# Edges behind a unit's latest add or operand for attention, rotation and weight pieces, and units' own steps issued first

## The chip, the cores and the metric

One core of a Trainium2 chip runs the whole program. The time is device microseconds of one execution. TensorE (PE) does the matrix products, VectorE (DVE) and ScalarE (ACT) the elementwise work, GpSimd (POOL) some of it and some transfers, and SyncE (SP) issues the other transfers. Each of these engines has its own list of instructions, fixed when the program is built, and works it off in that order.

## What is computed

Attention without a softmax, an RMS norm, a mixer that turns each value by an angle and mixes over tokens, and a two-part MLP, for 8 batches of 576 tokens with 512 features:

```python
kv = np.einsum('bhsd,bhse->bhde', k, v)
out = np.einsum('bhsd,bhde->bhse', q, kv)
x = out / np.sqrt(np.mean(out * out, axis=-1, keepdims=True) + 1e-06) * g_norm
...
theta = x @ w_theta
zr, zi = x * np.cos(theta), x * np.sin(theta)
y = einsum('ts,bsd->btd', w_tok_r, zr) + einsum('ts,bsd->btd', w_tok_i, zi)
u = x + y
u = u + np.maximum(u @ w_ch, 0.0)
...
h = np.maximum(u.transpose(0, 2, 1) @ w_tok1, 0.0) @ w_tok2
u = u + h.transpose(0, 2, 1)
out = u + np.maximum(u @ w_ch1, 0.0) @ w_ch2
```

## The kernel before

Every float32 product is made of three float16 products: both operands are split into a high part (`hi`, made by ACT) and a low part (`lo`, made by DVE from the value and `hi`), and `mm3` (L82 to L84) multiplies high by high, high by low and low by high into one PSUM bank.

The first 640 us go batch by batch. For a batch b the pieces are `attend(o, r)` for five row blocks r (attention output, norm, and the transposed copy that a DMA on SP's queue makes from `xs` into `xt`), `rotate(o, r)` (the angle product into `pt`, three sine steps on ACT with `cs`, the product of `cs` with x on DVE at L362, then `zh` on ACT and `zl` on DVE at L365 and L367; the fifth block, `rotate_last`, goes by `zt` and a DMA), then the units, which PE works on without a break: eight of `mix` (M, banks `py`, each followed by an add on DVE at L422, `uh` on ACT at L423 and `ul` on DVE at L426), eight of `channel` (C, banks `pr`, reading `uh` and `ul`; an add on DVE at L448, `xs` on ACT at L449 and on DVE at L456, and every second unit a transposing DMA `xt<-xs` at L460), four of `token1` (H, banks `ph`, reading that `xt`) and eight of `token2` (T, banks `pu`). A bank named py513 belongs to batch 5, second chunk of tokens (320 columns), fourth block of features. After that a blocked MLP (L82 to L84 with `pa` to `nc`) runs to the end; nothing in it is touched.

While the units of batch b run, the attention and rotation pieces of batch b+1 are strewn between them, and so are weight pieces: a float64 weight comes as pairs of 32-bit words, which ACT and three DVE steps turn into float32 (`decode`, L128 to L130), and `stash` splits it (L215, L217) and stores it.

The pieces are Python generators. `go` issues the first step of a new unit or piece after one further step of all that are pending. The framework's scheduler then decides the place of each instruction on its engine by its own timeline of costs, dependences and priorities. `urgent()` gives a unit's own adds and operands a higher priority; dependences of the kind NoSync order two instructions of one engine without a semaphore.

Of the kernel before, what the change touches and what calls it, by code (L numbers as in the profile page):

```python
# [13 lines left out]
AF = mybir.ActivationFunctionType  # L14
ALU = mybir.AluOpType
AX = mybir.AxisListType
# [12 lines left out]
def attn_mixer_kernel(  # L29
# [38 lines left out]
        nc.vector.scalar_tensor_tensor(lo, src, scale, hi, ALU.mult, ALU.subtract)  # L68

    def split_relu(hi, lo, src):  # L70
        nc.scalar.activation(hi, src, AF.Relu)
        nc.vector.scalar_tensor_tensor(lo, src, 0.0, hi, ALU.max, ALU.subtract)

    def urgent():

# [44 lines left out]
    def decode(val, raw):  # L120

        bits = val.bitcast(I32)
        first = nc.scalar.activation(val, raw[..., 1].bitcast(F32), AF.Copy, scale=2.0**-112)
        if wp:

            tc.keep_in_program_order(first)
        yield
        nc.vector.tensor_scalar(bits, bits, 3, None, ALU.logical_shift_left)  # L128
        nc.vector.scalar_tensor_tensor(bits, raw[..., 0], 29, bits, ALU.logical_shift_right, ALU.bitwise_or)
        nc.vector.scalar_tensor_tensor(bits, raw[..., 1], -(2**31), bits, ALU.bitwise_and, ALU.bitwise_or)  # L130

    def weight(pool, w, src, part, n, hi, lo, scale, name, raw=None):

# [52 lines left out]
    def stash(w, name, row, cols, dst):  # L186

        w, k = words(w)  # L190
        raw = wp[0].tile([P, 4, P, 2], I32, tag="raw", name=f"{name}r")
        if k == 1:
            raw = raw.rearrange("p x n w -> p x (n w)").bitcast(F32)[:, :, :P]
        for x, half in ((0, w.shape[1] // 2), (2, 0)):
            at = half + k * cols
            src = w.rearrange("(i r) n -> r i n", i=2)[row:row + P, :, at:at + k * P]
            load(raw[:, x:x + 2] if k == 1 else raw[:, x:x + 2].rearrange("p x n w -> p x (n w)"), src)

        for _ in range(7):
            yield  # L200
        t = wp[0].tile([P, 8, P], F32, tag="st", name=f"{name}s")
        if k == 1:
            nc.scalar.activation(t[:, :4], raw, AF.Copy)
        else:
            yield from decode(t[:, :4].rearrange("p x n -> p (x n)"), raw.rearrange("p x n w -> p (x n) w"))
        yield
        nc.gpsimd.tensor_tensor(t[:, 5], t[:, 0], t[:, 1], ALU.add)
        nc.gpsimd.tensor_tensor(t[:, 7], t[:, 0], t[:, 2], ALU.subtract)
        nc.gpsimd.tensor_tensor(t[:, 6], t[:, 5], t[:, 2], ALU.subtract)
        nc.gpsimd.tensor_tensor(t[:, 4], t[:, 3], t[:, 6], ALU.subtract)  # L210

        for _ in range(3):
            yield
        hi, lo = (wp[0].tile([P, 7, P], F16, tag=f"st{i}", name=f"{name}{i}", bufs=1) for i in range(2))
        tc.keep_in_program_order(nc.scalar.activation(hi, t[:, 1:], AF.Copy, scale=SW))  # L215
        yield
        nc.vector.scalar_tensor_tensor(lo, t[:, 1:], SW, hi, ALU.mult, ALU.subtract)  # L217
        yield
        yield
        for d, src in zip(dst, (hi, lo)):  # L220
            nc.gpsimd.dma_start(d, src)
# [61 lines left out]
    def attend(o, r):  # L283
# [13 lines left out]
        xt = o.xt[r] = fp.tile([P, 2, KD, P], F16, tag="xt", name=f"xt{b}{r}", bufs=NR + 1)  # L297

        x3 = x.rearrange("p (h d) -> p h d", d=D)
        yield  # L300
        nc.scalar.activation(x3, po3, AF.Square, scale=D**-0.5)
        yield
        nc.vector.tensor_reduce(ss, x3, axis=AX.X, op=ALU.add)
        nc.gpsimd.tensor_tensor(ss, ss, eps, ALU.add)
        nc.gpsimd.tensor_tensor(ri, ss, mhalf, ALU.pow)  # L305
        nc.gpsimd.tensor_tensor(
# [1 line left out]
        )  # L308
        yield
        yield  # L310
        nc.vector.tensor_tensor(x3, po3, x3, ALU.mult)
        n = SR if r == NR else P
        R = o.R[:, :, r * P:r * P + n]
        if b == 0:
# [6 lines left out]
            split(xt[:, 0], xt[:, 1], px, 1.0)  # L321
            nc.scalar.activation(R, px[:, :, :n], AF.Copy, scale=SW)
            return
        nc.scalar.activation(xs[:, 0, :], x, AF.Copy)
        yield
        nc.vector.tensor_tensor(xs[:, 1, :], x, xs[:, 0, :], ALU.subtract)  # L326
        nc.sync.dma_start_transpose(xt.rearrange("p a k t -> p (a k) t"), xs.rearrange("p a d -> p (a d)"))
        yield
        yield
        nc.scalar.activation(R, xt[:, 0, :, :n], AF.Copy, scale=SW)  # L330
        yield
        nc.vector.scalar_tensor_tensor(R, xt[:, 1, :, :n], SW, R, ALU.mult, ALU.add)

    def prepare(o):
        if o.zh is None:
# [4 lines left out]
    def rotate(o, r):  # L340

        b = o.b
        if r == 0:
            prepare(o)
        zh, zl, x, xt = o.zh, o.zl, o.x[r], o.xt[r]
        if r == NR:
            yield from rotate_last(o, xt)
            return
        pt = bank(f"pt{b}{r}")
        mm3(pt, [(xt[:, 0, kk, :], xt[:, 1, kk, :], wth[:, kk, :], wtl[:, kk, :]) for kk in range(KD)])  # L350

        cs = fp.tile([P, 2, DM], F32, tag="cs", name=f"cs{b}{r}", bufs=2)
        f, sn = cs[:, 0], cs[:, 1]
        yield
        nc.scalar.activation(f, pt, AF.Copy, bias=MAGIC)
        nc.vector.scalar_tensor_tensor(f, f, MAGIC, pt, ALU.subtract, ALU.subtract)
        yield
        nc.scalar.activation(sn, f, AF.Sin, scale=-RAD)
        nc.scalar.activation(f, f, AF.Abs)
        nc.scalar.activation(f, f, AF.Sin, bias=hpi, scale=-RAD)  # L360
        yield
        nc.vector.tensor_tensor(cs, cs, x.unsqueeze(1).to_broadcast([P, 2, DM]), ALU.mult)  # L362
        yield
        at = slice(r, r + NR + 1, NR)
        nc.scalar.activation(zh[:, at, :], cs, AF.Copy)  # L365
        yield
        nc.vector.tensor_tensor(zl[:, at, :], cs, zh[:, at, :], ALU.subtract)  # L367

    def rotate_last(o, xt):


        b = o.b
        pt = bank(f"pt{b}{NR}")[:, :KD * SR].rearrange("p (k t) -> p k t", k=KD)
        for dt in range(KD):
            ds = slice(dt * P, (dt + 1) * P)
            mm3(pt[:, dt, :], [(wth[:, kk, ds], wtl[:, kk, ds], xt[:, 0, kk, :SR], xt[:, 1, kk, :SR]) for kk in range(KD)])
        cs = fp.tile([P, 2, DM], F32, tag="cs", name=f"cs{b}{NR}", bufs=2)
        f = cs[:, 0, :KD * SR].rearrange("p (k t) -> p k t", k=KD)
        sn = cs[:, 1, :].rearrange("p (k i t) -> p k i t", k=KD, i=2)
        zt = fp.tile([P, 2, DM], F16, tag="xs", name=f"zt{b}", bufs=2)  # L380
        yield
        nc.scalar.activation(f, pt, AF.Copy, bias=MAGIC)
        nc.vector.scalar_tensor_tensor(f, f, MAGIC, pt, ALU.subtract, ALU.subtract)
        yield
        nc.scalar.activation(sn[:, :, 1, :], f, AF.Sin, scale=-RAD)
        nc.scalar.activation(f, f, AF.Abs)
        nc.scalar.activation(sn[:, :, 0, :], f, AF.Sin, bias=hpi, scale=-RAD)
        R = o.R[:, :, SM:]
        for i in range(2):
            nc.vector.scalar_tensor_tensor(sn[:, :, i, :], R, 1.0 / SW, sn[:, :, i, :], ALU.mult, ALU.mult)  # L390
        yield
        sn = sn.rearrange("p k i t -> p (k i t)")
        nc.scalar.activation(zt[:, 0, :], sn, AF.Copy)
        yield
        nc.vector.tensor_tensor(zt[:, 1, :], sn, zt[:, 0, :], ALU.subtract)
        nc.sync.dma_start_transpose(
            o.zh[:, KM - 1:, :].rearrange("p i (k d) -> p (i k) d", k=KD), zt.rearrange("p i n -> p (i n)")
        )


    def mix(o, c, dt):
# [17 lines left out]
        yield  # L419
        u = R[:, dt, cols]  # L420
        with urgent():
            nc.vector.tensor_tensor(u, py[0], u, ALU.add)  # L422
            nc.scalar.activation(uh[:, dt, :], u, AF.Copy, scale=1.0 / SW)  # L423
        yield
        with urgent():
            nc.vector.scalar_tensor_tensor(ul[:, dt, :], u, 1.0 / SW, uh[:, dt, :], ALU.mult, ALU.subtract)  # L426

    def channel(o, c, ct):
        b, R = o.b, o.R
# [15 lines left out]
        yield  # L445
        x2 = R[:, ct, cols]
        with urgent():
            nc.vector.scalar_tensor_tensor(x2, pr, 0.0, x2, ALU.max, ALU.add)  # L448
            nc.scalar.activation(xs[:, ct % 2, :n], x2, AF.Copy, scale=1.0 / SW)  # L449
        yield  # L450
        lows = [(slice(tiles * P, None), slice(0, 2 * P))]
        if n > 2 * P:
            lows.append((slice(n, tiles * P), slice(2 * P, n)))
        with urgent():
            for dst, at in lows:
                nc.vector.scalar_tensor_tensor(xs[:, ct % 2, dst], x2[:, at], 1.0 / SW, xs[:, ct % 2, at], ALU.mult, ALU.subtract)  # L456

            if ct % 2:
                m = tiles + 2
# [216 lines left out]
        return nxt  # L676


    pending = []

    def go(unit):
        advance()
        next(unit)
        pending.append(unit)

    def advance():
        for g in list(pending):
            try:
                next(g)
            except StopIteration:  # L690
                pending.remove(g)

    def flush():
        while pending:
            advance()

    extra = []
# [35 lines left out]
    TOKEN1 = [f"H{c}{i}" for c in range(2) for i in range(KJ)]  # L733
    UNITS = {"M": mix, "C": channel, "H": token1, "T": token2}

    def run(units, o, nxt, after, beside):

        for u in units:
            kind, c, i = u[0], int(u[1]), int(u[2])
            if kind == "K":  # L740
                front(kv, after, c)
            else:
                go(UNITS[kind](o, c, i))
            for what in beside.get(u, "").split():
                if what == "w":
                    spare()
                elif what == "l":
# [134 lines left out]
```

## Time and profile before

| | us |
|---|---|
| median of 3 runs | 1137.32 (1134.44 to 1139.80) |
| the profiled execution | 1135.75 |
| its span in the trace | 1134.0 |
| PE busy | 1078.6 (95%) |
| DVE busy | 839.6 (74%) |
| ACT busy | 563.0 (50%) |
| POOL busy | 231.9 (20%) |

The span reaches from the first instruction to the last one; the execution's time is 1.75 us more than that. The busy share is a mean over the start, the eight batches and the long MLP at the end, so it has to be read by stretches of time. The granted clock of PE is given as a share of 2.4 GHz: 1.00 is 2.4 GHz and 0.50 is 1.2 GHz.

### The profile page before, as it was taken

The numbers are of one execution on the slowest core, as the hardware profiler recorded it, in microseconds if no ns is written. First come the engines' busy times: TensorE is split into PE (matmuls) and PEld (weight loads), VectorE is DVE, ScalarE is ACT, GpSimd is POOL, SyncE is SP. The second block draws the span as 40 slices with busy tenths as digits, with TensorE's granted clock in tenths as the row PEclk, the third lists the DMA queues.
The fourth block names the chain that finished last, engine by engine and source line by source line (L and its number), as shares of the span: only waits on it lengthen the run. The fifth ranks groups of instructions, "written<-read, shape, count | busy, mean of one in ns | idle before, by whom it ended". The sixth has DMA issues, their size and how long they took to land.

```text
span 1134.0 us, 21659 instructions
## 1 busy us (share of the span) xinstructions
PE 1078.6 (95%) x8884; PEld 817.8 (72%) x8884; DVE 839.6 (74%) x1475; ACT 563.0 (50%) x958; POOL 231.9 (20%) x290
## 2 busy tenths in 40 slices
PE   3879999999998989989999999999999999999998
PEld 3556776676875767667677777777777777777776
DVE  4998777897887887978836494867768585848584
ACT  3766536355455464653623363636354544546361
POOL 2441052462652824527100000000000000000000
PEclk9789999999999999999999999999999999999999
DMA  9535474776747647763292802011010202020101
GB/s 323 201 129 112 108 198 107 213 185 138 210 121 201 179 116 201 170 152 102 45 279 53 310 1 84 2 42 43 32 53 17 69 12 74 12 74 1 43 1 42
DMA packets 146083, 126.35 MB, mean 111 GB/s; under 512 B 93184, under 2 KB 121984, under 8 KB 145984
## 3 DMA queue, kind: packets, MB, share of 16 engines
q1 hardware_dynamic: 140608, 104.53, 33.7%
q0 software_dynamic: 5376, 20.45, 5.1%
q8 instruction: 69, 1.13, 0.4%
q14 instruction: 30, 0.25, 0.1%
HBM read 74.29 MB, written 29.88 MB: 92 GB/s over the span
## 4 chain that ended last, share of the span: by engine, by line
PE 60%; DVE 20%; DMA 8%; ACT 6%; issue 3%; POOL 1%; SPq 1%; ACTq 0%; DVEq 0%
PE na L82 4%; PE na L84 4%; PE na L83 4%; PE pa L84 4%; PE pa L83 4%; PE pa L82 4%; DMA xt<-xs 4%; DVE xs L326 2%; PE nc L82 2%; PE nc L83 2%; PE pc L84 2%; PE pc L83 2%; PE pc L82 2%; PE nc L84 2%; DVE cs L362 2%
## 5 line engine op out<-in xcount | busy, mean ns | idle before, releaser
L82 PE MATMUL py<-wmh,zh 128*128 128x256 f16 (+1 forms) x576 | 166.3, 289 | 7.4 <-ACT zh L365 3.9
L83 PE MATMUL py<-wml,zh 128*128 128x256 f16 (+1 forms) x576 | 166.0, 288 | 0.0
L84 PE MATMUL py<-wmh,zl 128*128 128x320 f16 (+1 forms) x512 | 146.5, 289 | 3.9 <-DVE zl L367 3.9
L84 PE MATMUL na<-gh,wbl 128*128 128x288 f16 x384 | 109.3, 286 | 0.0
L83 PE MATMUL pa<-o,wah 128*128 128x288 f16 x384 | 109.2, 286 | 0.0
L83 PE MATMUL na<-gl,wbh 128*128 128x288 f16 x384 | 109.1, 286 | 0.0
L82 PE MATMUL pa<-o,wah 128*128 128x288 f16 x384 | 108.4, 286 | 0.0
L84 PE MATMUL pa<-o,wal 128*128 128x288 f16 x384 | 107.8, 286 | 0.0
L82 PE MATMUL na<-gh,wbh 128*128 128x288 f16 x384 | 106.0, 286 | 0.2
L82 PE MATMUL pr<-uh,wch 128*128 128x256 f16 (+1 forms) x256 | 75.9, 297 | 8.7 <-ACT uh L423 8.7
L566 DVE TENSOR_TENSOR gl<-sum,gh 128x1152 f16<-128x1152 f32 x48 | 65.0, 1354 | 21.9 <-ACT gh L565 21.9
L83 PE MATMUL pr<-ul,wch 128*128 128x256 f16 (+1 forms) x256 | 75.9, 296 | 5.4 <-DVE ul L426 5.3
L83 PEld LDWEIGHTS <-wbh 128*128 128x128 f16 x672 | 65.7, 98 | 17.8 <-issue 0.9
L82 PEld LDWEIGHTS <-wah 128*128 128x128 f16 x672 | 65.8, 98 | 16.6
L82 PEld LDWEIGHTS <-wbh 128*128 128x128 f16 x672 | 65.7, 98 | 16.6
L84 PEld LDWEIGHTS <-wal 128*128 128x128 f16 x672 | 65.8, 98 | 16.6
L83 PEld LDWEIGHTS <-wah 128*128 128x128 f16 x672 | 65.8, 98 | 16.6
L84 PEld LDWEIGHTS <-wbl 128*128 128x128 f16 x672 | 65.7, 98 | 16.6
L84 PE MATMUL pr<-uh,wcl 128*128 128x256 f16 (+1 forms) x256 | 76.1, 297 | 0.0
L82 PEld LDWEIGHTS <-zh 128*128 128x128 f16 x576 | 57.0, 99 | 24.4 <-ACT zh L365 4.8
L305 POOL TENSOR_TENSOR ri<-ss,mhalf 128x8 f32<-128x8 f32 x40 | 72.0, 1801 | 1.4
L83 PEld LDWEIGHTS <-zh 128*128 128x128 f16 x576 | 57.0, 99 | 15.9
(292 smaller groups left out, 2917.4 us busy)
## 6 DMA issues: line engine op xcount, KB each, us to landing
q<-in_q SPq DMA_DIRECT2D x8, 1152.0 KB, 7.8
c<-u2d SPq DMA_DIRECT2D x32, 288.0 KB, 4.2
out<-c SPq DMA_DIRECT2D x64, 144.0 KB, 1.8
k<-in_k SPq DMA_DIRECT2D x24, 256.0 KB, 5.7
v<-in_v SPq DMA_DIRECT2D x24, 256.0 KB, 6.0
wa_r<-in_w_ch SPq DMA_DIRECT2D x24, 256.0 KB, 3.7
wb_r<-in_w_ch SPq DMA_DIRECT2D x24, 256.0 KB, 3.9
wad<-wa POOLq DMA_DIRECT2D x24, 224.0 KB, 2.6
```

Of the source, the lines that this page charges most:

```text
L82: nc.tensor.matmul(acc, ah, bh, start=first and i == 0, stop=False, **more)
L83: nc.tensor.matmul(acc, ah, bl, start=False, stop=False, **more)
L84: nc.tensor.matmul(acc, al, bh, start=False, stop=last and i == n - 1, **more)
L305: nc.gpsimd.tensor_tensor(ri, ss, mhalf, ALU.pow)
L326: nc.vector.tensor_tensor(xs[:, 1, :], x, xs[:, 0, :], ALU.subtract)
L362: nc.vector.tensor_tensor(cs, cs, x.unsqueeze(1).to_broadcast([P, 2, DM]), ALU.mult)
L566: nc.vector.tensor_tensor(h.lo[:, 3:], h.s, h.hi[:, 3:], ALU.subtract)
```

## The change

Two small helpers are added. `lead` remembers, for each engine, the latest instruction that is a unit's own add or operand (L422, L423, L426, L448, L449, L456 and the relu of `token1`). `placed` gives an instruction a NoSync edge behind the one that `lead` remembers on the same engine. Pieces of attention and rotation of the batches after the first, and the weight pieces of all, go through `placed`. In `advance`, the units' own steps (`leading`) are issued before those of the pieces (`pending`), and pieces of the batches after the second yield once or twice more. No instruction is added or removed.

```diff
     def split_relu(hi, lo, src):
-        nc.scalar.activation(hi, src, AF.Relu)
-        nc.vector.scalar_tensor_tensor(lo, src, 0.0, hi, ALU.max, ALU.subtract)
+        lead(nc.scalar.activation(hi, src, AF.Relu))
+        lead(nc.vector.scalar_tensor_tensor(lo, src, 0.0, hi, ALU.max, ALU.subtract))
+
+    last = {}
+
+    def lead(ins):
+
+        last[ins.ins.engine] = ins.ins
+        return ins
+
+    def placed(ins):
+
+        prev = last.get(ins.ins.engine)
+        if prev is not None:
+            tc.add_manual_dep(
+                ins.ins, prev.name,
+                mybir.DependencyInfo(mybir.DependencyClass.NoSync, mybir.DependencyReason.DATA), reason="placed",
+            )
+        return ins
...
+        placed(nc.vector.tensor_scalar(bits, bits, 3, None, ALU.logical_shift_left))
...
-        nc.vector.scalar_tensor_tensor(lo, t[:, 1:], SW, hi, ALU.mult, ALU.subtract)
+        placed(nc.vector.scalar_tensor_tensor(lo, t[:, 1:], SW, hi, ALU.mult, ALU.subtract))
...
+        place = beside(o)
+        yield
+        place(nc.scalar.activation(x3, po3, AF.Square, scale=D**-0.5))
...
+        if b > 1:
+            yield
+        place(nc.scalar.activation(xs[:, 0, :], x, AF.Copy))
+        yield
+        place(nc.vector.tensor_tensor(xs[:, 1, :], x, xs[:, 0, :], ALU.subtract))
         nc.sync.dma_start_transpose(xt.rearrange("p a k t -> p (a k) t"), xs.rearrange("p a d -> p (a d)"))
...
+    def beside(o):
+        return placed if o.b else lambda ins: ins
...
+        place(nc.scalar.activation(f, pt, AF.Copy, bias=MAGIC))
+        if b > 1:
+            yield
+        place(nc.vector.scalar_tensor_tensor(f, f, MAGIC, pt, ALU.subtract, ALU.subtract))
...
-        nc.vector.tensor_tensor(cs, cs, x.unsqueeze(1).to_broadcast([P, 2, DM]), ALU.mult)
+        place(nc.vector.tensor_tensor(cs, cs, x.unsqueeze(1).to_broadcast([P, 2, DM]), ALU.mult))
...
-        nc.vector.tensor_tensor(zl[:, at, :], cs, zh[:, at, :], ALU.subtract)
+        place(nc.scalar.activation(zh[:, at, :], cs, AF.Copy))
+        yield
+        place(nc.vector.tensor_tensor(zl[:, at, :], cs, zh[:, at, :], ALU.subtract))
...
-            nc.vector.tensor_tensor(u, py[0], u, ALU.add)
-            nc.scalar.activation(uh[:, dt, :], u, AF.Copy, scale=1.0 / SW)
+            lead(nc.vector.tensor_tensor(u, py[0], u, ALU.add))
+            lead(nc.scalar.activation(uh[:, dt, :], u, AF.Copy, scale=1.0 / SW))
...
-    pending = []
-
-    def go(unit):
+    pending, leading = [], []
+
+    def go(unit, lead=False):
         advance()
         next(unit)
-        pending.append(unit)
+        (leading if lead else pending).append(unit)
 
     def advance():
-        for g in list(pending):
-            try:
-                next(g)
-            except StopIteration:
-                pending.remove(g)
+
+        for units in (leading, pending):
+            for g in list(units):
+                try:
+                    next(g)
+                except StopIteration:
+                    units.remove(g)
...
-                go(UNITS[kind](o, c, i))
+                go(UNITS[kind](o, c, i), True)
```

What this does to the lists of instructions shows at three places. Line numbers of the changed kernel are 17 to 33 higher than those of the kernel before (L453 is L422, L457 is L426, L479 is L448, L487 is L456, L388 is L362, L393 is L367).

**DVE in batch 5, from the add of py512 on.** R5 is the batch's running sum, ul51 the low operand of the second chunk, cs61 and cs62 are rotation blocks 1 and 2 of batch 6. Before:

```order
L422 TENSOR_TENSOR R5_4170<-py512_5598,R5_4170 128x320
L367 TENSOR_TENSOR zl6_5437<-cs61_5546,zh6_5436 128x2x512
L426 SCALAR_TENSOR_TENSOR ul51_5459<-R5_4170,uh51_5458 128x320
L356 SCALAR_TENSOR_TENSOR cs62_5648<-cs62_5648,pt62_5635 128x512
L362 TENSOR_TENSOR cs62_5648<-cs62_5648,x62_5263 128x1024
L422 TENSOR_TENSOR R5_4170<-py513_5653,R5_4170 128x320
L448 SCALAR_TENSOR_TENSOR R5_4170<-pr502_5687,R5_4170 128x256
L367 TENSOR_TENSOR zl6_5437<-cs62_5648,zh6_5436 128x2x512
L448 SCALAR_TENSOR_TENSOR R5_4170<-pr503_5707,R5_4170 128x256
L426 SCALAR_TENSOR_TENSOR ul51_5459<-R5_4170,uh51_5458 128x320
```

After:

```order
L453 TENSOR_TENSOR R5_4169<-py512_5596,R5_4169 128x320
L352 SCALAR_TENSOR_TENSOR R6_5078<-xt64_5364,R6_5078 128x4x64
L388 TENSOR_TENSOR cs61_5543<-cs61_5543,x61_5125 128x1024
L457 SCALAR_TENSOR_TENSOR ul51_5455<-R5_4169,uh51_5454 128x320
L453 TENSOR_TENSOR R5_4169<-py513_5651,R5_4169 128x320
L393 TENSOR_TENSOR zl6_5434<-cs61_5543,zh6_5433 128x2x512
L382 SCALAR_TENSOR_TENSOR cs62_5647<-cs62_5647,pt62_5634 128x512
L457 SCALAR_TENSOR_TENSOR ul51_5455<-R5_4169,uh51_5454 128x320
L479 SCALAR_TENSOR_TENSOR R5_4169<-pr502_5684,R5_4169 128x256
L479 SCALAR_TENSOR_TENSOR R5_4169<-pr503_5706,R5_4169 128x256
```

The product of cs62 with x and the low part zl6 from it no longer stand ahead of the add of py513 and the low operand made from it; they come eight rows further down, as the next piece shows.

**DVE and SP in batch 5, from the add of pr510 on.** The `xs` pieces feed the transposing transfers that `token1`'s second half reads; zt6 is the fifth rotation block of batch 6. DVE before:

```order
L448 SCALAR_TENSOR_TENSOR R5_4170<-pr510_5815,R5_4170 128x320
L390 SCALAR_TENSOR_TENSOR cs64_5774<-R6_5079,cs64_5774 128x4x64
L456 SCALAR_TENSOR_TENSOR xs510_5814<-R5_4170,xs510_5814 128x256
L456 SCALAR_TENSOR_TENSOR xs510_5814<-R5_4170,xs510_5814 128x64
L448 SCALAR_TENSOR_TENSOR R5_4170<-pr511_5838,R5_4170 128x320
L395 TENSOR_TENSOR zt6_5775<-cs64_5774,zt6_5775 128x512
L456 SCALAR_TENSOR_TENSOR xs510_5814<-R5_4170,xs510_5814 128x256
L456 SCALAR_TENSOR_TENSOR xs510_5814<-R5_4170,xs510_5814 128x64
L448 SCALAR_TENSOR_TENSOR R5_4170<-pr512_5854,R5_4170 128x320
L456 SCALAR_TENSOR_TENSOR xs512_5853<-R5_4170,xs512_5853 128x256
L456 SCALAR_TENSOR_TENSOR xs512_5853<-R5_4170,xs512_5853 128x64
```

DVE after (it begins with the row ahead of the add of pr510):

```order
L388 TENSOR_TENSOR cs62_5647<-cs62_5647,x62_5263 128x1024
L479 SCALAR_TENSOR_TENSOR R5_4169<-pr510_5810,R5_4169 128x320
L479 SCALAR_TENSOR_TENSOR R5_4169<-pr511_5835,R5_4169 128x320
L393 TENSOR_TENSOR zl6_5434<-cs62_5647,zh6_5433 128x2x512
L487 SCALAR_TENSOR_TENSOR xs510_5809<-R5_4169,xs510_5809 128x256
L487 SCALAR_TENSOR_TENSOR xs510_5809<-R5_4169,xs510_5809 128x64
L421 SCALAR_TENSOR_TENSOR cs64_5773<-R6_5078,cs64_5773 128x4x64
L487 SCALAR_TENSOR_TENSOR xs510_5809<-R5_4169,xs510_5809 128x256
L479 SCALAR_TENSOR_TENSOR R5_4169<-pr512_5852,R5_4169 128x320
L487 SCALAR_TENSOR_TENSOR xs510_5809<-R5_4169,xs510_5809 128x64
L421 SCALAR_TENSOR_TENSOR cs64_5773<-R6_5078,cs64_5773 128x4x64
L479 SCALAR_TENSOR_TENSOR R5_4169<-pr513_5872,R5_4169 128x320
```

SP before, around the transfers to xt51:

```order
L246 DMA v74_5811<-in_v 96x512
L116 DMA wb41_r_5831<-in_w_ch2 128x2x256 x2
L396 DMA_TRANSPOSE zh6_5436<-zt6_5775 128x8x128
L460 DMA_TRANSPOSE xt51_5813<-xs510_5814 128x10x128
L460 DMA_TRANSPOSE xt51_5813<-xs512_5853 128x10x128
L116 DMA wb50_r_5926<-in_w_ch2 128x2x256 x2
```

SP after, the same place:

```order
L263 DMA v74_5806<-in_v 96x512
L133 DMA wb41_r_5828<-in_w_ch2 128x2x256 x2
L491 DMA_TRANSPOSE xt51_5808<-xs510_5809 128x10x128
L427 DMA_TRANSPOSE zh6_5433<-zt6_5774 128x8x128
L491 DMA_TRANSPOSE xt51_5808<-xs512_5851 128x10x128
L133 DMA wb50_r_5925<-in_w_ch2 128x2x256 x2
```

On DVE the product and low part of cs62 now stand beside the adds of pr510 and pr511, and the two cs64 rows a little lower; on SP the transfer from zt6 now goes between the two from xs510 and xs512, ahead of both of which it stood.

**DVE at the start, where the rotation of batch 0 ends and the attention of batch 1 begins.** zt0 is the fifth rotation block of batch 0, py000 the first `mix` bank, x10 to x14 the attention rows of batch 1, xs10 the source of the first transposing transfer of batch 1, wc0 weight pieces. Before:

```order
L311 TENSOR_TENSOR x12_774<-po12_766,x12_774 128x512
L303 TENSOR_REDUCE ss13_832<-x13_835 128x8
L395 TENSOR_TENSOR zt0_513<-cs04_512,zt0_513 128x512
L326 TENSOR_TENSOR xs10_660<-x10_661,xs10_660 128x512
L303 TENSOR_REDUCE ss14_895<-x14_898 128x8
L311 TENSOR_TENSOR x13_835<-po13_827,x13_835 128x512
L311 TENSOR_TENSOR x14_898<-po14_890,x14_898 128x512
L326 TENSOR_TENSOR xs11_714<-x11_715,xs11_714 128x512
L332 SCALAR_TENSOR_TENSOR R1_652<-xt10_662,R1_652 128x4x128
L326 TENSOR_TENSOR xs12_773<-x12_774,xs12_773 128x512
L422 TENSOR_TENSOR R0_212<-py000_622,R0_212 128x256
```

After:

```order
L421 SCALAR_TENSOR_TENSOR cs04_512<-R0_212,cs04_512 128x4x64 x2
L426 TENSOR_TENSOR zt0_513<-cs04_512,zt0_513 128x512
L453 TENSOR_TENSOR R0_212<-py000_622,R0_212 128x256
L453 TENSOR_TENSOR R0_212<-py001_673,R0_212 128x256
L145 TENSOR_SCALAR wc0_0v_665<-wc0_0v_665 128x512
L453 TENSOR_TENSOR R0_212<-py002_732,R0_212 128x256
L145 TENSOR_SCALAR wc0_1v_722<-wc0_1v_722 128x512
L457 SCALAR_TENSOR_TENSOR ul00_621<-R0_212,uh00_620 128x256
L453 TENSOR_TENSOR R0_212<-py003_793,R0_212 128x256
L146 SCALAR_TENSOR_TENSOR wc0_0v_665<-wc0_0r_666,wc0_0v_665 128x512
L321 TENSOR_REDUCE ss10_658<-x10_661 128x8
L457 SCALAR_TENSOR_TENSOR ul00_621<-R0_212,uh00_620 128x256
```

Before, the reductions, products and weight steps of batch 1 up to x12 stood ahead of zt0, and xs10 right behind it, ahead of the add of py000. Now zt0 comes before all of batch 1's rows, and the add of py000 and 24 further rows (adds, `ul`, weight steps, five reductions ss10 to ss14, x10 and x11) come between zt0 and xs10.

## Rows read from the trace of the kernel before

**Rows 1.** The head of the profile page: span, and busy time of each engine.

```profile
span 1134.0 us, 21659 instructions
PE 1078.6 (95%) x8884; PEld 817.8 (72%) x8884; DVE 839.6 (74%) x1475; ACT 563.0 (50%) x958; POOL 231.9 (20%) x290
```

**Rows 2.** The last stretch: busy time of each engine, granted clock, DMA share.

```profile
648.00:1134.00 486.00, 482.37 (x3931) 384.25 (x3928) 335.67 (x603) 234.71 (x369) 0.00 (x0) 1.00 0.11 37
```

**Rows 3.** PE's waits from 108 to 600 us: total, times, longest.

```profile
PE pr L82 <- ACT uh L423: 8.7, 5, 2.7
PE pr L83 <- DVE ul L426: 5.3, 4, 1.3
PE py L82 <- DMA zh<-zt: 2.5, 1, 2.5
PE ph L476 <- DMA xt<-xs: 2.3, 2, 1.9
```

**Rows 4.** PE in order of time: start, length, in brackets the wait before it.

```profile
90.73 0.38 PE L82 MATMUL pt<-wth,xt 128*128 128x512 f16 x1
...
207.40 0.39 PE L476 MATMUL ph<-xt,w1h 128*128 128x512 f16 x1 [1.94 <-DMA xt<-xs]
...
483.33 0.30 PE L84 MATMUL py<-wmh,zh 128*128 128x320 f16 x1
...
491.41 0.30 PE L82 MATMUL pr<-uh,wch 128*128 128x320 f16 x1 [1.36 <-ACT uh L423]
...
493.05 0.30 PE L83 MATMUL pr<-ul,wch 128*128 128x320 f16 x1 [1.34 <-DVE ul L426]
...
505.47 0.39 PE L476 MATMUL ph<-xt,w1h 128*128 128x512 f16 x1 [0.38 <-DMA xt<-xs]
...
566.24 0.69 PE L82 MATMUL pr<-uh,wch 128*128 128x320 f16 x2 [2.11 <-ACT uh L423]
```

**Rows 5.** DVE in order of time, batch 5: start, length, wait before.

```profile
446.64 2.56 DVE L326 TENSOR_TENSOR xs<-x,xs 128x512 f16<-128x512 f32 x1 [0.30 <-ACT xs L324]
...
488.69 1.23 DVE L362 TENSOR_TENSOR cs<-cs,x 128x1024 f32<-128x1024 f32 x1 [2.11 <-ACT cs L360]
489.83 0.48 DVE L422 TENSOR_TENSOR R<-py,R 128x320 f32<-128x320 f32 x1
...
492.51 0.48 DVE L426 SCALAR_TENSOR_TENSOR ul<-R,uh 128x320 f16<-128x320 f32 x1
...
501.34 0.56 DVE L456 SCALAR_TENSOR_TENSOR xs<-R,xs 128x256 f16<-128x256 f32 x2 [0.54 <-ACT xs L449]
```

**Rows 6.** ACT in order of time, at the start and in batch 5.

```profile
90.03 0.63 ACT L330 ACTIVATE R<-xt 128x512 f32<-128x512 f16 x1 [0.35 <-DMA xt<-xs]
...
490.91 0.45 ACT L423 ACTIVATE uh<-R 128x320 f16<-128x320 f32 x1
```

**Rows 7.** Three short stretches: PE busy first, granted clock third from the end.

```profile
136.10:139.51 3.41, 3.41 (x18) 2.43 (x17) 1.76 (x6) 1.19 (x3) 0.00 (x0) 0.50 0.80 198
...
566.18:569.59 3.41, 3.27 (x12) 1.68 (x12) 2.45 (x7) 0.84 (x3) 0.00 (x0) 0.50 0.53 88
491.40:494.80 3.40, 2.05 (x14) 1.36 (x14) 3.40 (x7) 1.79 (x4) 1.06 (x2) 1.00 0.24 90
```

**Rows 8.** SP's queue in order of time: start, length of the issue.

```profile
84.44 1.34 SPq L396 DMA_TRANSPOSE zh<-zt  x1
85.88 2.26 SPq L327 DMA_TRANSPOSE xt<-xs  x1
...
498.43 1.23 SPq L396 DMA_TRANSPOSE zh<-zt  x1
499.77 3.54 SPq L460 DMA_TRANSPOSE xt<-xs  x2
```

**Rows 9.** DVE in order of time at the start.

```profile
83.74 0.68 DVE L395 TENSOR_TENSOR zt<-cs,zt 128x512 f16<-128x512 f32 x1
84.34 0.69 DVE L326 TENSOR_TENSOR xs<-x,xs 128x512 f16<-128x512 f32 x1
84.95 0.67 DVE L303 TENSOR_REDUCE ss<-x 128x8 f32<-128x512 f32 x1
...
93.50 0.42 DVE L128 TENSOR_SCALAR wc_2v<-wc_2v 128x512 int32<-128x512 int32 x1
93.84 0.75 DVE L422 TENSOR_TENSOR R<-py,R 128x256 f32<-128x256 f32 x2
```

## What the change will do to the time

> **What bounds the kernel now.** I read the page's head first: PE is busy for 1078.6 of the 1134.0 us span [rows 1], so about 55 us is all that PE stands idle. The last stretch, from 648 us on, holds only 3.6 us of idle PE at a granted clock of 1.00 [rows 2], and the change touches nothing in it. So all that counts lies in the first 600 us. The table of PE's waits there names four: 8.7 us of `pr` on `uh`, 5.3 on `ul`, 2.5 of `py` on a transfer from `zt`, 2.3 of `ph` on a transfer from `xs` [rows 3]. The first two are one place per batch: the fifth `channel` unit, the first of the second chunk.
>
> The timelines of batch 5 tell why. PE ends py513 at about 483.6 and needs it as the operand of the last quarter of pr510, which could run at 491.41 - 1.36 = 490.05 but starts at 491.41 and stops again until 493.05 [rows 4]. DVE adds py513 only at 489.83, six microseconds after it is there, since in front of the add stands the product of cs62, which sat 2.11 us waiting for ACT's sine chain and then took 1.2 [rows 5]. ACT's `uh` follows at 490.91 [rows 6], DVE's `ul` at 492.51 [rows 5]. So a unit's own add queues behind a piece of the next batch that nobody needs yet. The four steady places (266 to 494 us) cost PE 14.0 - 2.1 = 11.9 us: 8.7 and 5.3 summed [rows 3], less the 2.11 at 566.24 that belongs to batch 6 [rows 4].
>
> Idle time costs a second time. From 108 to 600 us six stretches of 3.41 us run at a granted clock of 0.50, the level of 1.2 GHz, the first at 136.10 and the last at 566.18, each right after a wait; the wait at 491 us was followed by none [rows 7]. Half speed for 3.41 us is 1.7 us lost. Three of the four steady places pay it: 5.1 us, so those places cost 17.0 us. The period of a batch is (505.47 - 207.40)/4 = 74.5 us [rows 4].
>
> **Part one, the steady batches.** Nothing is added; rows trade places. The product of cs62 and its `zl` go behind the add of pr510 and of pr511. Walking DVE's new list with the old durations from py512's add (483.0 at the earliest): the product of cs61 to 485.0, py513's add to 485.8, `uh` on ACT to 486.4, then the `zl` of cs61 (1.2) and the sine step of cs62 (0.7) and `ul` until 488.3. PE asks for `ul` of py513 first at 490.05 or later, so both waits go, with two microseconds to spare: 11.9 us and the three half-clock stretches, 17.0.
>
> But something is late next. The moved rows now stand among the adds of pr510 to pr513, whose `xs` parts feed the transfers that the second half of `token1` waits for. Before, the last `xs` part began at 501.34 [rows 5], the second of the two transfers was issued in the stretch that began at 499.77 and took 3.54 with both [rows 8], and PE came to it 0.38 us too early [rows 4]. After, PE is there 2.7 us sooner, at 502.4. My walk puts the last `xs` part 1.6 us sooner only (two rows of 1.2 us are in its way, but the adds no longer wait), done about 500.3. On SP the transfer from zt6 now goes between the two, where it was ahead of both; it holds the queue for 1.23 us [rows 8]. Landing then falls near 504.5. So PE waits 2.1 us at `ph`, four times: 8.4 us, with bounds of 0 (the rows slip into gaps of DVE) and 4.2 (the wait removed comes back whole, clock included). Whether the clock drops after such a wait, the trace leaves open: 1.94 us at 207.40 [rows 4] was followed by half clock, the 2.7 us in two parts at 491 were not [rows 7]. I take two of four: 3.4 us. Gain: 17.0 - 8.4 - 3.4 = 5.2 us, from 0 to 17.
>
> **Part two, batch 6.** The wait of 2.11 us at 566.24 [rows 4] with its half clock [rows 7] has the same cause, the fifth rotation block ahead of py613's add, and that block now comes behind it. No further rotation is queued there to be late. Gain 2.1 + 1.7 = 3.8, at worst 0.
>
> **Part three, batch 1.** The wait of 1.94 us at 207.40 [rows 4] and its half clock, 3.6 us, are those of the `ph` transfers, once. They may shrink as the adds are less late, or stay: 0.7, from 0 to 3.6.
>
> **Part four, the start.** This part speaks against the change. zt0, done at 84.4 [rows 9], is now free of batch 1's rows; by my walk it is done at 75.6 and lands about 80.1, 4.5 later like the one issued at 84.44 [rows 8]. PE uses it at once. But xs10, the first source of batch 1, done at 85.0 [rows 9], now stands behind py000's add, which cannot run before 80.6, and 24 more rows: nine of 0.34 us, thirteen of 0.6 and two of 0.4 make 11.7; with that add and xs10 itself 12.7, so xs10 is done near 93.5. The distances 83.74, 84.34, 84.95 and 93.50, 93.84 give these prices [rows 9]. Its transfer, issued at 85.88 [rows 8], was there for ACT at 90.03 [rows 6], 4.15 later; now it lands near 97.9. PE has nothing else at that place in its list than pt10, which began at 90.73 [rows 4]: it starts 7.2 later, after some 11 idle microseconds, with half clock behind it (1.7). In return PE is later against DVE, so the 2.5 us of `py` on `zt` [rows 3] at 135 and its half clock [rows 7] should go: 4.2 back. Net loss 7.2 + 1.7 - 4.2 = 4.7; bounds 0 (the rows run beside PE's remaining units, should DVE reach them sooner) and 10.5 (8.8 late, the clock, and nothing back).
>
> **Sum.** 5.2 + 3.8 + 0.7 - 4.7 = 5.0 us gained, set against the profiled execution of 1135.75 (span 1134.0 and 1.75 around it): 1130.8. The median of the runs, 1137.32, lies 1.6 above that execution; I place the result between the two scales, at 1132.
>
> A rule that speaks against the change is weighed here by itself. In the rows, xs60's low part took 2.56 us at 446.64 where its like takes 0.69 [rows 5, 9]; POOL was at work beside it. The Trainium skill says (SBUF — State Buffer, Who interferes with whom) that VectorE and GpSimd share one pair of SBUF ports under an exclusive lock, so that the loser stands still for the whole of the other's instruction. The long row agrees with it. By the rule each of the two moved rows in batch 5, which read two SBUF operands, could stand still for one POOL instruction, where the sum has them at their undisturbed 1.2 us; the rival below that ends slower is what it would make.
>
> **Rivals.** *No second wait.* If the moved rows fall into DVE's gaps and the transfers are in time, PE is the bound in the steady batches and the whole 17.0 is won: 17.0 + 3.8 + 1.9 - 4.7 = 18, a time of 1118 to 1120. For it: the adds of pr510 to pr513 now wait 0.54 us at a time for ACT [rows 5], and the queue on DVE was late, not full. Against it: SP's order, which costs 1.2 us by itself.
>
> *The wait only changes its name.* If the `ph` transfers come as late as the `uh` did, four times 4.2, the steady gain is 0, and 3.8 - 4.7 is left, about -1: 1137 to 1138. For it: the two sums are near each other, and DVE does the same work.
>
> *The start decides, slower.* The place is pt10 on PE. Each microsecond that xs10 is late is one of PE, since nothing stands in PE's list that could run. With DVE rows stretched like the 2.56 us one [rows 5] between py000's add and xs10, three such rows add 5.6 us, and the loss is 10.5 or more with nothing back at 135; if the moved rows of the steady batches are stretched likewise the `ph` wait takes the steady gain whole: 3.8 - 10.5 = -6.7, 1144. It decides from xs10 done later than 97 us together with a `ph` wait above 4 us. Against it: near 90 us the rows of the same kind took 0.69 [rows 9]. By the Trainium skill (SBUF — State Buffer, Who interferes with whom) this would be the shared port pair at work.
>
> **How the numbers follow.** 0.5% of the median is 5.7 us, about what a measurement of this kernel tells from no change. Forecast (1126 to 1136): 0.45. No second wait: 0.2. The wait changes its name: 0.2. The start decides: 0.15. The forecast's own 0.45 lies around the border of 1131.6, a little over half above it: 0.2 faster, 0.25 same. Faster: 0.2 + 0.2 and 0.02 of the rest, 0.42; slower: 0.14 of the last case; same 0.44. The range reaches from 1117 to 1144: it takes in the first rival's time and the last rival's, and leaves 2 in 10 outside.
>
> **What would show it.** Right: no wait of `pr` on `uh` or `ul` above 0.5 us in batches 2 to 6; the add of py513 less than 3 us behind py513's end; a new wait of `ph` on `xt<-xs` of 1 to 3 us per batch, period 72.5 to 74; a wait of `pt` on `xt<-xs` of 8 to 13 us near 86 us; no wait of `py` on `zt` at 130 to 140 us. Wrong: the `pr` waits stay (then the walk of DVE's list missed who is late), or `pt` waits less than 4 us at the start (then the fourth part falls and the time is near 1127), or the `ph` wait is 4 us and more.

## The result, and the profile after

The changed kernel takes 1124.67 us (median of 4 runs, 1124.40 to 1125.93) against 1135.88 of the kernel before (4 runs, one more than in the table above): a ratio of 0.990, 95% interval 0.9869 to 0.9931. It is faster, by 11 us where 5 were forecast. The time is inside the range of 1117 to 1144, but below the band of 1126 to 1136 that the forecast itself was given. The spans of the two profiled executions differ by 1134.0 - 1122.6 = 11.4 us.

The head of the page after, then the last stretch of the windows view:

```profile
span 1122.6 us, 21649 instructions
PE 1067.5 (95%) x8884; PEld 813.4 (72%) x8884; DVE 830.6 (74%) x1475; ACT 560.1 (50%) x958; POOL 230.1 (20%) x290
```

```profile
648.00:1122.60 474.60, 471.03 (x3838) 375.12 (x3836) 325.04 (x583) 224.85 (x351) 0.00 (x0) 1.00 0.11 36
```

Against [rows 1] the first surprise stands here: PE's idle time is what it was, 1122.6 - 1067.5 = 55.1 us after and 55.4 before. What shrank by 11.1 us is the busy time of the same 8884 matmuls. The last stretch is full, as in [rows 2].

PE's waits after, some of those up to 108 us and from there to 600 (line, what it waited for, total, times, longest; where several things end a wait, the view names the one that came last):

```profile
PE pt L99 <- DMA xt<-xs: 12.0, 1, 12.0
...
PE ph L507 <- DMA xt<-xs: 5.1, 5, 2.9
PE ph L507 <- DVE xs L487: 1.9, 2, 1.2
PE pu L101 <- DVE hl L72: 1.0, 2, 0.6
PE pu L99 <- ACT hh L71: 0.6, 1, 0.6
PE py L99 <- DMA zh<-zt: 0.6, 1, 0.6
...
PE ph L507 <- DVE cs L421: 0.4, 1, 0.4
```

The `pr` waits of [rows 3] are gone without a rest, `ph` waits instead (7.4 us in its three rows, most of it for its transfers), and one wait of 12.0 us has come at the start. PE in order of time, with the wait in brackets, and two short stretches of the windows view (granted clock third from the end):

```profile
97.47 0.61 PE L99 MATMUL pt<-wth,xt 128*128 128x512 f16 x1 [11.96 <-DMA xt<-xs]
...
222.78 0.27 PE L99 MATMUL py<-wmh,zh 128*128 128x256 f16 x1
...
355.66 0.39 PE L507 MATMUL ph<-xt,w1h 128*128 128x512 f16 x1 [2.86 <-DMA xt<-xs]
...
508.52 0.27 PE L99 MATMUL py<-wmh,zh 128*128 128x256 f16 x1
```

```profile
88.15:101.80 13.65, 4.33 (x11) 1.55 (x12) 10.41 (x18) 5.30 (x10) 12.59 (x11) 0.50 0.66 187
355.66:359.07 3.41, 3.41 (x16) 1.64 (x17) 0.84 (x2) 0.60 (x1) 0.00 (x0) 1.00 0.92 272
```

The longest of the new `ph` waits, 2.86 us, was followed by a clock of 1.00. After the wait for pt10, PE ran at 0.50 until 101.80.

DVE in order of time, batch 5, the place of [rows 5] (L453 adds py513 at 478.72, L457 makes `ul`, L388 and L393 are the product of cs62 and its `zl`):

```profile
478.72 0.48 DVE L453 TENSOR_TENSOR R<-py,R 128x320 f32<-128x320 f32 x1
479.25 1.23 DVE L393 TENSOR_TENSOR zl<-cs,zh 128x1024 f16<-128x1024 f32 x1
480.40 0.68 DVE L382 SCALAR_TENSOR_TENSOR cs<-cs,pt 128x512 f32<-128x512 f32 x1
480.99 0.48 DVE L457 SCALAR_TENSOR_TENSOR ul<-R,uh 128x320 f16<-128x320 f32 x1
...
485.50 1.23 DVE L388 TENSOR_TENSOR cs<-cs,x 128x1024 f32<-128x1024 f32 x1 [0.61 <-ACT cs L386]
486.64 0.88 DVE L479 SCALAR_TENSOR_TENSOR R<-pr,R 128x320 f32<-128x320 f32 x2
487.85 1.23 DVE L393 TENSOR_TENSOR zl<-cs,zh 128x1024 f16<-128x1024 f32 x1 [0.33 <-ACT zh L391]
```

py513's operands are whole at 481.5 (480.99 and 0.48); PE begins pr510 at 482.60. Where DVE stood still 2.11 us for the sine chain, it now stands 0.61.

How far PE is ahead or behind at the first matmul of some banks (before, after and difference, from both traces with PE's list named in order):

```
bank     before   after    diff
py000     53.92    54.67   +0.75
pt10      90.73    97.47   +6.74
py011     93.33   102.19   +8.86   pt10's wait and its half clock
py103    137.42   141.98   +4.56   the wait on zt1 is gone
py110    160.89   167.10   +6.21   token2 of batch 0 waits for hh, hl
py200    220.21   222.78   +2.57   ph of batch 1 waits no more
py600    516.60   508.52   -8.08   four steady batches
py700    573.28   561.17  -12.11   batch 6
pa00     635.35   624.01  -11.34   the MLP begins
```

### The profile page after: what moved, and what is told of

Read it like the earlier page. It is cut to its first block, busy times and chain, and to the rows that moved or that the text cites. A ratio compares the mean times of both kernels' runs of the same rounds, so it can differ in the third digit from the quotient of the medians.

```text
span 1122.6 us, 21649 instructions
## 1 busy us (share of the span) xinstructions
PE 1067.5 (95%) x8884; PEld 813.4 (72%) x8884; DVE 830.6 (74%) x1475; ACT 560.1 (50%) x958; POOL 230.1 (20%) x290
## 4 chain that ended last, share of the span: by engine, by line
PE 63%; DVE 17%; DMA 7%; ACT 5%; issue 4%; POOL 3%; SPq 1%; ACTq 0%; DVEq 0%; POOLq 0%
PE na L99 4%; PE na L101 4%; PE pa L101 4%; PE pa L99 4%; PE na L100 4%; PE pa L100 4%; PE py L101 2%; PE py L99 2%; PE py L100 2%; PE pc L99 2%; PE nc L100 2%; PE pc L101 2%; PE nc L101 2%; PE pc L100 2%; PE nc L99 2%
## 5 line engine op out<-in xcount | busy, mean ns | idle before, releaser
L99 PE MATMUL py<-wmh,zh 128*128 128x320 f16 (+1 forms) x576 | 164.7, 287 | 1.7 <-ACT zh L391 1.0
L100 PE MATMUL py<-wml,zh 128*128 128x320 f16 (+1 forms) x576 | 164.7, 287 | 0.0
L323 POOL TENSOR_TENSOR ri<-ss,mhalf 128x8 f32<-128x8 f32 x40 | 79.1, 1979 | 1.6
L99 PE MATMUL pr<-uh,wch 128*128 128x256 f16 (+1 forms) x256 | 73.1, 286 | 0.0
L100 PE MATMUL pr<-ul,wch 128*128 128x256 f16 (+1 forms) x256 | 73.0, 286 | 0.0
L101 PE MATMUL pr<-uh,wcl 128*128 128x256 f16 (+1 forms) x256 | 73.0, 286 | 0.0
L99 PEld LDWEIGHTS <-zh 128*128 128x128 f16 x576 | 56.6, 98 | 17.6 <-ACT zh L391 1.2
L596 ACT ACTIVATE gh<-sum 128x1152 f16<-128x1152 f32 x48 | 55.5, 1156 | 25.5 <-DVE sum L644 25.5
```

The lines of the kernel that those rows point to most:

```text
L99: nc.tensor.matmul(acc, ah, bh, start=first and i == 0, stop=False, **more)
L100: nc.tensor.matmul(acc, ah, bl, start=False, stop=False, **more)
L101: nc.tensor.matmul(acc, al, bh, start=False, stop=last and i == n - 1, **more)
L596: nc.scalar.activation(h.hi[:, 3:], h.s, AF.Copy)
```

## The experiments

Each ratio is to runs of the kernel before on the same chip (its medians there: 1135.88 to 1137.23 us), so kernels are best compared by their ratios. Period and "still" come from one profiled execution of each kernel. "Period" is the way from batch 2's first matmul to batch 6's, divided by four; "still" is how long DVE stood idle ahead of the product of `cs` (its idle column in the groups view) from 210 to 570 us.

```
kernel              median   ratio (95% interval)     period  still
before                                                 74.1    14.6
one_edge            1134.0   0.998 (0.9965 to 0.9998)  74.9    13.3
rot_edges_bare      1129.1   0.993 (0.990 to 0.995)    74.0    12.0
issue_only          1127.0   0.991 (0.988 to 0.994)    73.1    14.0
no_yields           1127.1   0.992 (0.990 to 0.995)    71.4     6.7
rot_only            1122.7   0.988 (0.985 to 0.990)    71.2     4.0
edges_only          1121.5   0.987 (0.983 to 0.990)    70.9     5.9
changed kernel      1124.7   0.990 (0.987 to 0.993)    71.4     2.6
start_free          1120.3   0.986 (0.982 to 0.990)    71.4     2.6
zt_behind           1119.2   0.985 (0.982 to 0.988)    70.4     2.6
edges_free_behind   1117.6   0.982 (0.979 to 0.985)    70.6     5.1
free_and_behind     1115.3   0.982 (0.979 to 0.985)    70.4     2.6
```

**start_free: is the start's loss real, and what is given back?**

```diff
-        return placed if o.b else lambda ins: ins
+        return placed if o.b > 1 else lambda ins: ins
...
-        if prev is not None:
+        if prev is not None and wp:
```

> The changed kernel with the start undone: batch 1's attention and rotation and the first weight pieces go without edges, everything from batch 2 on as changed. Queue theory (the start costs because batch 1's first source xs10 stands behind batch 0's adds on VectorE): the 12.0 us wait of pt on its transfer near 97 us goes, 8.1 us come back there, the wait on zt1 near 135 us and its half clock (4.3 us) return: 1119 to 1121. Rival (the start's loss is made up later whatever is done at the start): 1124 to 1126.

1120.3, as expected. On DVE zt0 and xs10 stand as before the change, the `pt` wait is gone, and pt10 begins at 90.0. The wait on zt1 is back, 2.75 us, with a half-clock stretch:

```profile
135.17 0.28 PE L99 MATMUL py<-wmh,zh 128*128 128x256 f16 x1 [2.75 <-DMA zh<-zt]
```

The intervals of the two kernels overlap, but the traces show both parts of the exchange, as the queue theory had them.

**edges_only and issue_only: which half of the change does it?** edges_only appends every generator to `pending`, as before the change; issue_only lets `placed` do nothing.

```diff
-        (leading if lead else pending).append(unit)
+        pending.append(unit)
```

```diff
-        prev = last.get(ins.ins.engine)
+        prev = None
```

> The changed kernel with one list of pending generators in the order of before: the edges and the extra yields alone. Queue theory: the add of py513 is ahead of the product of cs62 here too, so the waits of pr on uh and ul are gone and the start's loss stays: 1123 to 1128. Rival (what counts is that units' own steps are issued first): most of the 11 us is lost, 1131 or more.

> The changed kernel without any edge: only the order of issue and the extra yields. TensorE's list is the one of before, and on VectorE the product of cs62 stays ahead of the add of py513. Queue theory: the pr waits stay at 12 to 14 us, the start is as before: 1133 to 1138. Rival (the order of issue carries part of the gain): 1131 or less.

edges_only: 1121.5, somewhat below its expectation, so the edges with the yields carry the steady gain alone. issue_only: 1127.0, where the queue theory said 1133 to 1138; the rival was right there. Its `pr` waits are 7.6 us in place of 14.0, and the add of py510 starts 5.2 us behind its bank's end where it was 7.4, so the yields and the order of issue shorten DVE's queue somewhat by themselves, though the product of cs62 stays ahead of py513's add. DVE's idle time ahead of the product is 14.0 us here, as good as before: that idle time alone does not set the period. The waits of issue_only from 210 to 600 us:

```profile
PE pr L100 <- DVE ul L457: 5.7, 5, 1.3
PE ph L507 <- DMA xt<-xs: 5.4, 4, 2.1
PE pr L99 <- ACT uh L454: 1.9, 3, 1.1
```

**one_edge: is it that one row?** The kernel before, with only the product of cs on block 2 moved behind the latest `mix` add:

```diff
...
-            nc.vector.tensor_tensor(u, py[0], u, ALU.add)
+            lead(nc.vector.tensor_tensor(u, py[0], u, ALU.add))
...
+        place = placed if b > 1 and r == 2 else lambda ins: ins
-        nc.vector.tensor_tensor(cs, cs, x.unsqueeze(1).to_broadcast([P, 2, DM]), ALU.mult)
+        place(nc.vector.tensor_tensor(cs, cs, x.unsqueeze(1).to_broadcast([P, 2, DM]), ALU.mult))
```

> The kernel before with one edge per batch and nothing else of the change: the product of cs on rotation block 2 (batches 3 to 6 move) goes behind the latest add of a mix unit on VectorE; TensorE's list is untouched and four pairs of rows trade places on VectorE. Queue theory: the add of py513 no longer sits behind the sine chain, the 11.9 us of pr waits and the 5.1 us of half clock go, and 1 to 2 us of ph wait come per batch: 1123 to 1129 against 1136.4 before. Rival (the gain comes from many pieces together, a single row is worth little): 1132 to 1136.

1134.0, two microseconds, as the rival had it, and the period did not fall at all. The `pr` waits went to 3.4 us as the prediction's walk of the list would have it; but `ph` took their place, with half clock at three of these waits:

```profile
PE ph L494 <- DMA xt<-xs: 9.3, 4, 3.3
PE ph L494 <- DVE R L466: 3.8, 3, 1.3
PE pr L99 <- ACT uh L441: 2.1, 2, 1.3
PE pr L100 <- DVE ul L444: 1.3, 2, 1.0
```

This is the prediction's second rival, "the wait only changes its name", and for one row it is the truth. How late each add starts behind the end of its bank shows where the debt goes (us, mean of batches 2 to 5, from the traces):

```
bank    before  one_edge  rot_edges_bare  changed
py510      7.4       7.0             7.1      2.9
py513      6.5       3.1             3.3      1.6
pr500      7.1       7.0             7.3      3.5
pr503      6.2       5.5             5.7      2.0
pr510      2.3       4.1             4.1      2.7
pr513      0.7       3.3             3.7      2.1
```

Moved by one place, the row pays for py513 with pr510 to pr513, and these feed the transfers. In the changed kernel DVE is less behind than before from py510 to pr503; at pr510 and pr513 it is more behind than before (2.7 and 2.1 where it was 2.3 and 0.7), but less than in one_edge.

**rot_only, no_yields, rot_edges_bare: what do the edges need?** rot_only keeps the edges of rotation alone; no_yields takes the `if b > 1` yields out; rot_edges_bare has rotation's edges (from batch 2 on), no yields, one list. The first piece below is from rot_only, the second from no_yields, both cut.

```diff
-        place = beside(o)
+        place = lambda ins: ins
...
-        placed(nc.vector.tensor_scalar(bits, bits, 3, None, ALU.logical_shift_left))
+        (nc.vector.tensor_scalar(bits, bits, 3, None, ALU.logical_shift_left))
```

```diff
-        if b > 1:
-            yield
...
```

> The changed kernel with the edges of attention and weight pieces taken away, those of the rotation kept. At the start zt0 then stands as before the change. Queue theory: only rotation rows wait for long chains, so the steady batches gain as in start_free, and the start costs nothing: 1117 to 1122. Rival (the weight and attention rows ahead of adds cost as much): 1124 or more.

> The changed kernel without the extra yields of batches after the second. The add of py513 is still ahead of the product of cs62. Theory: the yields matter little, the start's loss is in: 1121 to 1126. Rival (without them the pr waits return in part): 1128 or more.

> The kernel before with edges on the rotation pieces of the batches after the second alone: no extra yields, one list, attention and weights free. TensorE's list is the one of before. Theory of the standstill (VectorE must not stand still for the sine chain with adds behind it; an edge only reaches back to the latest add that was issued, which without yields or a leading list is too early): VectorE's idle time ahead of the product of cs stays above 10 us in 210 to 570 us, and the time is near one_edge, 1130 to 1135. Rival (edges on all rotation rows are enough by themselves): 1121 to 1126, and that idle time is under 6 us.

1122.7, 1127.1 and 1129.1: the first two fall between their two expectations and decide nothing by their times, the third falls just under its own, with the idle time of 12.0 us that was expected. The periods say more. Rotation's edges do the steady part (71.2 in rot_only), attention's and the weights' add nothing that shows. Yields or a leading list, one of the two is enough for the period (70.9 in edges_only, 71.4 in no_yields). Bare, the edges leave it at 74.0: an edge goes to the latest add that was traced, and without yields or a leading list that is an earlier one, so that the product stands close behind py513's add, as in one_edge (the add at 479.97 and the product at 482.16; 486.36 and 488.55 in one_edge). The idle column of DVE's group of the product (busy and mean ns, then idle before it and what ended it), 210 to 570 us, before, rot_edges_bare and the changed kernel:

```profile
L362 DVE TENSOR_TENSOR cs<-cs,x 128x1024 f32<-128x1024 f32 x21 | 25.7, 1223 | 14.6 <-ACT cs L360 14.4
```

```profile
L384 DVE TENSOR_TENSOR cs<-cs,x 128x1024 f32<-128x1024 f32 x20 | 25.2, 1262 | 12.0 <-ACT cs L382 11.5
```

```profile
L388 DVE TENSOR_TENSOR cs<-cs,x 128x1024 f32<-128x1024 f32 x21 | 26.6, 1267 | 2.6 <-ACT cs L386 2.6
```

What rot_edges_bare does gain against before lies outside the steady batches: 3.7 us up to py200, most of it at batch 1's `ph`, and 4.0 from py600 to pa00.

**zt_behind, free_and_behind, edges_free_behind: is the new wait SyncE's order, and do the two losses add?**

```diff
+        if b > 1:
+            yield
+            yield
-        nc.sync.dma_start_transpose(
+        place(nc.sync.dma_start_transpose(
             o.zh[:, KM - 1:, :]...
...
-                nc.sync.dma_start_transpose(
+                lead(nc.sync.dma_start_transpose(
                     xt[:, (ct - 1) * m:(ct + 1) * m, :], xsf
...
```

> The changed kernel with one more edge: the transposing transfer from zt goes behind the second transfer from xs of the batch before it on SyncE, for batches 2 to 6. Theory of the new wait (the transfer from zt holds SyncE for 1.23 us ahead of the transfer that ph's second half waits for): the ph waits of the second half, 1.04, 2.86 and 0.40 us, shrink by up to 1.23 each: 1121.5 to 1123.5. Rival (VectorE's last xs part is what is late, or the transfers' landing): 1124 to 1126.

> start_free and zt_behind together: batch 1 and the first weights without edges, and the transfer from zt behind both transfers from xs on SyncE. If the two losses are separate, as both theories say, their gains add: 1120.3 less 4 to 5.4, 1113 to 1117. Rival (one hides the other, since the later place has slack only because the start was late): 1119 to 1121.

> free_and_behind with one list of pending generators (edges_only's order of issue). On SyncE the edge of the zt transfer then binds one step earlier: it stands between the two transfers from xs, no longer ahead of both. If the order of issue is worth nothing once the edges are there (edges_only's batches took 70.9 us, the changed kernel's 71.4): 1112 to 1117, as free_and_behind. Rival (the order of issue is needed for the zt edge to bind behind both): 1116 to 1120, as start_free.

The edit of zt_behind adds two yields along with its edge. It took 1119.2, more gain than was expected. SyncE's queue in order of time, the changed kernel and then zt_behind, batch 5:

```profile
490.81 1.33 SPq L491 DMA_TRANSPOSE xt<-xs  x1
492.58 1.23 SPq L427 DMA_TRANSPOSE zh<-zt  x1
493.92 1.36 SPq L491 DMA_TRANSPOSE xt<-xs  x1
```

```profile
486.42 3.53 SPq L494 DMA_TRANSPOSE xt<-xs  x2
490.01 1.49 SPq L430 DMA_TRANSPOSE zh<-zt  x1
```

All that PE then waits for from 210 to 600 us is this, against 8.0 us in the changed kernel:

```profile
PE ph L510 <- DMA xt<-xs: 3.4, 6, 1.3
```

At `token1`'s second half, which the edge is about, the waits fell from 4.6 to 1.9 us. Why those at its first half fell too, from 2.8 to 1.5, is not shown.

free_and_behind adds both, 1115.3, below the interval of the changed kernel and the best here: 20 us under the kernel before. edges_free_behind, 1117.6, lies just above its own expectation and inside the rival's, but its ratio is that of free_and_behind, 0.982: it settles nothing on the order of issue.

## Why the prediction was right, and where its sizes were not

**Part one, the steady batches: right in kind, half the size.** Forecast 5.2 us of gain, measured 2.57 + 8.08 = 10.65. The `pr` waits went, as walked, and py513's add now starts 1.6 us behind its bank's end. The new `ph` wait was put at 8.4 us, all of it at `token1`'s second half; from 270 to 500 us it is 7.4, of which 4.6 lie at the second half and 2.8 at the first, where the walk had none. What failed is the term for the clock: two drops of four, 3.4 us, were charged to the new waits, and none came. Nor did one come in the seven other kernels with a period under 72 us: in no trace of theirs does a stretch between 162 and 1100 us run at 0.50, while each of the four slower kernels has one to five. In full: 17.0 - 7.4 = 9.6, and the `ph` wait of 0.38 us that was there before is in the 7.4, which makes 10.0. From py200 to py600 the two traces split the 10.65 evenly: PE stands idle 12.7 us before and 7.4 after, and is busy 283.7 and 278.4. Over the whole run PE's idle total is unchanged, since the idle time saved in the batches (about 10 us) was given back at the start; so what remains of the gain is time at 1.2 GHz that is no longer spent. The period, put at 72.5 to 74, came out at 71.4.

The cause was told too narrowly. The prediction put the stall down to the row of cs62 in front of one add; one_edge took just that row away and the wait came back whole under `ph`. What the edges, with yields or a leading list, do is that DVE, which works in order, no longer stands still for ACT's chains with adds behind it: 14.6 us of idle ahead of the product, 2.6 after. The Trainium skill says the same of the queues (PSUM — Partial Sum Buffer, Engine vs sequencer instructions: those of ScalarE, VectorE and GpSimd are strict first in, first out). These idle times agree with it. With the chains met later, the adds from py510 to pr503 all start sooner behind their banks, not the one of py513 alone. DVE does not stand still less in all. Its busy time from 210 to 570 us (the third figure after the length; the kernel before, then the changed one) is nearly the same, so the idle time now lies in other places:

```profile
210.00:570.00 360.00, 345.11 (x2898) 251.19 (x2897) 300.54 (x494) 189.47 (x337) 169.06 (x219) 0.98 0.58 153
210.00:570.00 360.00, 352.02 (x3051) 260.36 (x3051) 299.21 (x512) 193.22 (x347) 171.22 (x223) 1.00 0.62 162
```

The standstill ahead of the product is not the whole cause: issue_only, with 14.0 us of it, still won 1.0 us a batch, and no_yields, with 6.7, has the changed kernel's period.

**Part two, batch 6**: 3.8 forecast, 12.11 - 8.08 = 4.0 measured, and 0.8 is lost again in batch 7, where `py` waits 0.6 for zt7's transfer, whose source on DVE now stands behind more of the `xs` pieces.

**Part three, batch 1**: 0.7 forecast, 6.21 - 2.57 = 3.6 measured, the upper bound: the whole wait and its half clock went. rot_edges_bare, with rotation's edges alone, has no wait there either.

**Part four, the start: right in each row that it names.** xs10 was to be done at 93.5 and was at 94.3; pt10 was to start 7.2 us later, at 97.9, and started at 97.47; wait 11, measured 11.96; the clock's 1.7 was 2.1 (8.86 - 6.74); 4.2 back at 135 us, measured 4.3. Left out were the waits of `pu` on `hh` and `hl` in batch 0, 1.6 us, which start_free does not have; why the late start brings them was not tried. Net 6.2 against 4.7 (0.75 of it lies ahead of py000).

xs10 was 0.8 us later than walked, and two long rows stand ahead of it. DVE after, then POOL:

```profile
86.94 1.52 DVE L147 SCALAR_TENSOR_TENSOR wc_1v<-wc_1r,wc_1v 128x512 int32<-128x512 int32 x1
...
90.60 1.52 DVE L169 SCALAR_TENSOR_TENSOR wcl<-wc_1v,wch 128x512 f16<-128x512 f32 x1
92.05 0.48 DVE L457 SCALAR_TENSOR_TENSOR ul<-R,uh 128x320 f16<-128x320 f32 x1
```

```profile
86.70 1.22 POOL L324 TENSOR_TENSOR x<-ri,gb 128x512 f32<-128x512 f32 x1
...
90.09 1.49 POOL L324 TENSOR_TENSOR x<-ri,gb 128x512 f32<-128x512 f32 x1
91.54 2.08 POOL L323 TENSOR_TENSOR ri<-ss,mhalf 128x8 f32<-128x8 f32 x1
```

Two rows that take 0.69 elsewhere took 1.52, together 1.7 us more; each began while POOL's product (L324) ran and ended 0.5 us behind it. The Trainium skill's exclusive lock (SBUF — State Buffer, Who interferes with whom) would do just that; these two rows agree with it, but no run took POOL's rows away. It does not show beside every row of POOL: the `ul` at 92.05, which also reads two operands in SBUF, took its usual 0.48 us wholly beside L323. The rival built on the lock, the start deciding for slower, did not come: two rows, not many. In the steady batches the moved products were hardly longer (mean 1.27 us after, 1.22 before).

**The sum**: 5.2 + 3.8 + 0.7 - 4.7 = 5.0 forecast; 10.65 + 3.25 + 3.65 - 6.2 = 11.3 measured. The range held, but no case in it was the one that came: 1124.67 lies between the forecast's band and the 1118 to 1120 of the rival "no second wait". That rival was half true: the wait is there, and without its clock it costs somewhat over two fifths of what it replaced.

## What to carry to other kernels

When an in-order engine delivers late, moving the row just ahead of the late one only hands the delay to the next; look at how late each row starts behind what it reads, and where the engine stands still for others' chains with due rows behind, and give those chains room by more steps between them. Order edges bind to what was traced before; here they needed more steps or a leading list to bind to the right add. Where an edge holds back work of the next stage, look at the point where that stage starts with nothing else to run: there the edges are better left out (start_free).

## Not expected of the hardware

How long PE waited does not by itself say whether its clock falls. one_edge has two waits of the same kind and length, and the stretches behind them (PE in order of time, then the windows view, granted clock third from the end):

```profile
280.70 0.39 PE L494 MATMUL ph<-xt,w1h 128*128 128x512 f16 x1 [2.15 <-DMA xt<-xs]
...
357.61 0.39 PE L494 MATMUL ph<-xt,w1h 128*128 128x512 f16 x1 [2.14 <-DMA xt<-xs]
```

```profile
280.99:284.40 3.41, 3.41 (x10) 1.23 (x9) 1.65 (x2) 1.87 (x5) 0.61 (x2) 0.50 1.02 340
357.61:361.02 3.41, 3.41 (x16) 1.64 (x17) 1.92 (x2) 1.60 (x3) 0.00 (x0) 1.00 1.00 317
```

After the first PE ran at 0.50, after the second at 1.00. It also ran at 1.00 after the 2.86 us in the changed kernel, while 1.94 us in the kernel before [rows 4] were followed by 0.50. What else decides stays open. In the changed kernel no stretch from 108 us to the end of the batches ran at 0.50, in the kernel before six did.
